# Value bursts of a sliding-window attention kernel: one PSUM bank per array half and step, summed at the evacuation

## The chip, the cores and the metric

The kernel runs on one core of one Trainium2 chip. The metric is the device time of one execution in microseconds; of each kernel the median of several runs is given. A profiled execution has its own time, and its span (first to last instruction) is a little shorter than that.

## What is computed

```python
def _A_ref(x, wqkv, wo):                 # 32 heads of 16, window of 256 keys
    qkv = (x @ wqkv).reshape(B, S, 3, H, Dh).transpose(2, 0, 3, 1, 4)
    q, k, v = qkv[0], qkv[1], qkv[2]
    scores = jnp.einsum("bhqd,bhkd->bhqk", q, k) * (Dh ** -0.5)
    mask = (idx[:, None] - idx[None, :] >= 0) & (idx[:, None] - idx[None, :] < W)
    p = _softmax(jnp.where(mask[None, None], scores, -1e9), axis=-1)
    o = jnp.einsum("bhqk,bhkd->bhqd", p, v)
    return o.transpose(0, 2, 1, 3).reshape(B, S, D) @ wo

def _B_ref(x, w_gate, w_up, w_down):
    h = _sigmoid(x @ w_gate) * (x @ w_up)
    return h @ w_down

g = _sigmoid((x * gate_w).sum(-1, keepdims=True))
out = g * _A_ref(x, wqkv, wo) + (1 - g) * _B_ref(x, w_gate, w_up, w_down)
```

x is 2048 x 512 in fp32, the gated branch has 1376 hidden columns.

## The kernel before

The heads are worked in NG = 8 groups of four, the 2048 queries in NB = 16 blocks of 128. The main loop at L902 counts units u, one block of one group each; a step s is four blocks of queries (512) of one group, so a group has the steps c = 0 to 3. In each unit and for each head hh of the four, TensorE gets, in this order:

- `s_part` (L361): scores of query block u, into a PSUM tile `s`; VectorE adds the mask and takes the row maxima (L377);
- `st_part` (L429): transposed scores of the block nine units earlier, into a tile `st`; ScalarE takes the exponential (L443) into `pbuf` or `V`, the homes of the block's probabilities, and GpSimd masks them (L450, L456);
- a turn or several of `turns` (L754): a pair of matmuls, one on either half of the array, of the projections (`pj`), the gated branch (`gu`) or its tail (`tp`).

Most matmuls use 64 of the array's 128 rows, so that two run side by side, one on the lower half (partitions 0 to 63) and one on the upper. PSUM has eight banks: two with the tag `s`, two with `st`, three with `misc`, and `pv`. A tag's banks are handed out in turn, and an engine's instructions stand in the order in which the code records them; the recording layer adds the waits.

Probabilities times values are done in bursts. From unit 17 on there is a long visit each eight units (`visits`, L895; 14 in all, the last at u = 121), at the head of its unit, ahead of `s_part(u, 0)`. It does two steps, s and s + 1. For each key block j, `pv_row` (L482) issues one matmul per head on one half of the array (`half`: the lower or upper 64 keys), with 32 columns of the array per head; a key block meets only the queries of its window, so a row is 64 to 320 columns wide. The sum over j stands in a bank, and both halves add to the same step's bank. `pv_wide` (L498) keeps them apart in time: in the first phase (`turn` 0) the lower half works for step s in bank `pv` and the upper half for step s + 1 in a bank of tag `st`; then TensorE is drained, and in the second phase the halves change banks. One half takes its key blocks backwards, so that the rows that run side by side have like sizes.

While the burst runs, ScalarE and VectorE do other things that are due (L977 to L988: evacuations, the split of two projections in high and low parts, up to five guests). Behind it ScalarE copies the second step's bank to `pbuf[:, 26:28]` (`o_copy`, L526), and, after the first exponential of the unit, the first step's bank to `pbuf[:, 24:26]`; `o_store` (L529) queues five transfers of them. Slots 24 to 29 of `pbuf` are also the home of the probabilities of each block with u % 8 = 4 (`p_home`, L408). The last group's steps have short visits (`pv_part`, L465), which the change leaves alone.

Of the kernel before, what the change touches and what calls it, by code (L numbers as in the profile page):

```python
# [7 lines left out]
F32 = mybir.dt.float32  # L8
# [3 lines left out]
ALU = mybir.AluOpType  # L12
PSUM = bass.MemoryType.PSUM

P = 128
HB = P // 2
# [7 lines left out]
CH = 512  # L24
NC = T // CH
# [41 lines left out]
def gated_mix_kernel(  # L67
# [11 lines left out]
    nc = tc.nc  # L79
# [30 lines left out]
    ps = ctx.enter_context(tc.tile_pool(name="ps", bufs=1, space=PSUM))  # L110
# [34 lines left out]
    with ExitStack() as actx:  # L145
# [316 lines left out]
        evac = []  # L462
# [19 lines left out]
        def pv_row(s, half, j, bank, first):  # L482
            g, c = divmod(s, NC)
            q0 = 8 * c
            a = 2 * j + half
            k, e = max(a, q0) - 2 * j, min(a + 5, q0 + 8) - 2 * j
            for hh in range(HG):
                v = (j * HG + hh) * VW
                w = min(32, NB * HG * VW - v)
                o = (2 * j - q0) * HB  # L490
                mm(  # L491
                    bank[32 * hh:32 * hh + w, o + k * HB:o + e * HB],
                    vt[HB * half:HB * half + HB, v:v + w], p_run(g * NB + j, hh, half, k, e),
                    start=first, stop=False, skip_group_check=True, tile_position=(HB * half, 32 * hh),
                )
            return e - k

        def pv_wide(s, banks):  # L498
            for turn in range(2):
                rows = []  # L500
                for half in range(2):
                    n = (half + turn) % 2
                    c = (s + n) % NC
                    js = list(range(max(0, 4 * c - 2), 4 * c + 4))
                    rows.append([(s + n, half, j, banks[n]) for j in (js if half != turn else js[::-1])])
                sent = [0, 0]
                began = [False, False]
                while rows[0] or rows[1]:
                    half = 0 if rows[0] and (not rows[1] or sent[0] <= sent[1]) else 1
                    row = rows[half].pop(0)  # L510
                    n = pv_row(*row, turn == 0 and not began[half])
                    began[half] = True
                    sent[half] += n
                if turn == 0:
                    nc.tensor.drain()

        def o_take(s, bank):
            g, c = divmod(s, NC)
# [4 lines left out]
                later.append((oT_d[h * DH:(h + 1) * DH, c * CH:(c + 1) * CH], ob[32 * hh:32 * hh + DH]))  # L523
            later.append((sum_d[c, g * HG:(g + 1) * HG], ob.rearrange("(h r) f -> r h f", r=32)[DH]))

        def o_copy(half, bank):  # L526
            nc.scalar.copy(pbuf[:, 24 + 2 * half:26 + 2 * half].rearrange("p c h t -> p (c h t)"), bank)

        def o_store(s):  # L529
            g, c = divmod(s, NC)  # L530
            both = pbuf[:, 24:28].rearrange("p c h t -> p (c h t)")
            for hh in range(HG):
                h = g * HG + hh
                later.append((oT_d[h * DH:(h + 1) * DH, c * CH:(c + 2) * CH], both[32 * hh:32 * hh + DH]))
            later.append((
                sum_d[c:c + 2, g * HG:(g + 1) * HG].rearrange("c h f -> h c f"),
                both.rearrange("(h r) (c f) -> r h c f", r=32, c=2)[DH],
            ))
# [175 lines left out]
        def proj_sum(s):  # L714
# [12 lines left out]
                lambda k, h=None, x=False, a=(f, c, w): gu_mm(*a, k, h, x),  # L727
# [174 lines left out]
        for u in range(N):  # L902
            if u == LAG:
# [3 lines left out]
                pbuf = ppool.tile([P, 30, HG, HB], F32, name="pbuf")  # L907
# [51 lines left out]
            for hh in range(HG):  # L959
                wide = visits.get(u) == 2  # L960
                if hh == 0 and u in visits:
                    s2 = (u - PVLAG) // 4 - wide
                    if wide:
                        second = ps.tile([P, CH], F32, tag="st", name=f"pv{s2}", bufs=2)
                        pv_wide(s2, (pv, second))
                    else:
                        pv_part(s2, pv)
                if hh == 3 and mid(u + 1):
                    max_split((u - 4) // 4)
                if hh == 0 and mark:  # L970
                    if not mid(u):
                        max_split((u - 5) // 4)
                    run_dmas(later)
                    later.clear()
                    max_store((u - 5) // 4)
                if hh == 0 and wide:
                    flush(evac)  # L977
                    ripe = [held.pop(0) for _ in range(2) if held and held[0] // 2 == u // 8 + 1]
                    for s4 in ripe:
                        proj_hi(s4)  # L980
                    max_load((u - 5) // 4)
                    for s4 in ripe:
                        proj_lo(s4)
                    run_dmas(later)
                    later.clear()
                    for guests, n in ((acts, 2), (behind, 3)):
                        for _ in range(min(n, len(guests))):
                            guests.pop(0)()  # L988
                    o_copy(1, second)
                    evac.append(lambda s2=s2: (o_copy(0, pv), o_store(s2)))  # L990
                elif hh == 0 and u in visits:
                    evac.append(lambda s2=s2: o_take(s2, pv))
                if hh == 2 and mark:
                    transfers()
                if u < NU:
                    s_part(u, hh)
                if 0 <= u - LAG < NU:
                    st_part(u - LAG, hh ^ 1 if u < NU else hh)
                if u < LAG:
                    flush(behind)  # L1000
                    if hh % 2 == 1:
                        upto = n_first * (2 * u + 1 + hh // 2) // (2 * LAG)
                        run_first(upto - done)
                        done = upto
                else:
                    long = u < U_WIDE
                    k8 = (u - LAG) % WIDE * HG + hh
                    dense = GAPS2[max(0, k8 - 1)] < 3 if long else u < NU and (u - PVLAG) % 4 == 3 and hh > 0
                    k = (u - PVLAG) % 4 * HG + hh
                    free = hh == 2 and not mid(u + 1) if long else k in (1, 5, 9) or k in (3, 7) and len(behind) > 2  # L1010
                    guest = behind and (u < PVLAG or u >= NU or free)
                    if guest:
                        behind.pop(0)()
                    if evac and not (NB * NWIDE + LAG <= u < NU and (guest or hh == 3 and mid(u + 1))):
                        evac.pop(0)()
                    elif acts and not dense and (u < NU or hh % 2 == 1):
                        acts.pop(0)()
                if u >= LAG and (hh % 2 == 1 or u < NU) and (u + 1 not in visits or hh < HG - 1):
                    if u < N - 2:
                        next(slots)  # L1020
# [204 lines left out]
```

## Time and profile before

| | |
|---|---|
| median of 3 runs | 717.32 us (717.19 to 717.95) |
| the profiled execution | 716.68 us, span 714.9 us |
| granted TensorE clock, mean | 1.000 |
| TensorE matmuls busy | 707.9 us (99%) |
| TensorE weight loads busy | 608.4 us (85%) |
| VectorE busy | 478.8 us (67%) |
| ScalarE busy | 426.8 us (60%) |
| GpSimd busy | 172.0 us (24%) |

The profile comes from one execution. PE stands for TensorE's matmuls, PEld for its weight loads, DVE for VectorE, ACT for ScalarE, POOL for GpSimd, SP for the queue that issues the transfers. Matmuls are pipelined: a matmul's row lasts longer than the time it adds to the stream, so starts are to be compared, not durations summed. "q" behind an engine's name is its sequencer.

### The profile page before, as it was taken

The page shows a single profiled execution, that of the slowest core. Times are in us where ns is not written, and L with a number is a line of the kernel's source. Part 1 is how long each engine was busy: PE and PEld are TensorE (multiplying, and loading weights), DVE is VectorE, ACT ScalarE, POOL GpSimd, SP SyncE. Part 2 cuts the span into 40 slices and gives each one's busy share as a digit, 9 for nine tenths or more (in the row PEclk, how much of TensorE's full clock was granted, in tenths as well). Part 3 has the DMA queues.
Part 4 walks back from the last instruction along what each step waited for, and adds up shares of the span by engine and source line. Part 5 has one row for each costly group of instructions (what it writes and reads, how often), then busy time and mean ns, then how long its engine had stood idle before and what let it go on. Part 6 is the DMA issues. An engine that isn't in the chain of part 4 may idle for free.

```text
span 714.9 us, 19859 instructions
## 1 busy us (share of the span) xinstructions
PE 707.9 (99%) x7530; PEld 608.4 (85%) x7530; DVE 478.8 (67%) x1455; ACT 426.8 (60%) x890; POOL 172.0 (24%) x254
## 2 busy tenths in 40 slices
PE   9999999999999999999999999999999999999997
PEld 7888889889898898888988888898888888888886
DVE  5368767667676676766667667676747858667481
ACT  6423767667676676766767667775676645435341
POOL 5200333233233233323324323332341000000000
PEclk9999999999999999999999999999999999999999
DMA  8466644635445365462655617564569968779531
GB/s 305 115 192 200 212 130 173 222 128 192 160 171 190 125 206 175 158 210 96 213 166 183 208 49 244 182 230 115 167 207 268 254 177 219 190 188 236 146 65 59
DMA packets 102975, 127.37 MB, mean 178 GB/s; under 512 B 45766, under 2 KB 62662, under 8 KB 102880
## 3 DMA queue, kind: packets, MB, share of 16 engines
q1 hardware_dynamic: 102736, 125.98, 58.0%
q8 instruction: 59, 0.97, 0.6%
q14 instruction: 36, 0.29, 0.1%
q10 hardware_dynamic: 144, 0.13, 0.1%
HBM read 71.80 MB, written 51.13 MB: 172 GB/s over the span
## 4 chain that ended last, share of the span: by engine, by line
PE 99%; issue 0%; DVE 0%; DVEq 0%
PE gu L283 28%; PE pj L283 12%; PE pv L491 9%; PE s L371 6%; PE st L436 6%; PE tp L661 6%; PE pd L96 5%; PE pd L97 5%; PE pd L95 5%; PE vh L698 4%; PE pa L95 2%; PE pa L97 2%; PE pa L96 2%; PE vps L560 2%; PE pv L474 1%; PE pd L1152 1%
## 5 line engine op out<-in xcount | busy, mean ns | idle before, releaser
L377 DVE CUSTOM_DVE_ANT_0 junk<-s,mask 128x384 f32<-128x384 f32 (+2 forms) x512 | 271.8, 531 | 133.7 <-PE s L371 71.5
L283 PE MATMUL gu<-xh,w 64*128 64x512 f32 x1152 | 271.4, 391 | 0.0
L443 ACT ACTIVATE pbuf<-st 128x384 f32<-128x384 f32 (+2 forms) x344 | 166.3, 492 | 70.4 <-PE st L436 38.8
L283 PE MATMUL gu<-xl,w 64*128 64x512 f32 x576 | 183.1, 389 | 0.0
L436 PE MATMUL st<-ring 64*128 64x384 f32 (+2 forms) x536 | 165.6, 326 | 0.0
L371 PE MATMUL s<-ring 64*128 64x384 f32 (+2 forms) x536 | 163.1, 322 | 0.0
L283 PEld LDWEIGHTS gu<-xh,w 64*128 64x128 f32 x1152 | 153.2, 184 | 6.5
L450 POOL TENSOR_SCALAR_AFFINE_SELECT pbuf<-pbuf 128x512 f32<-128x512 f32 x86 | 58.1, 676 | 277.9 <-ACT pbuf L443 247.6
L371 PEld LDWEIGHTS s<-ring 64*128 64x128 f32 x536 | 94.9, 184 | 15.7 <-issue 3.1
L436 PEld LDWEIGHTS st<-ring 64*128 64x128 f32 x536 | 95.5, 184 | 4.0 <-PE pv L474 0.4
L443 ACT ACTIVATE V<-st 128x384 f32<-128x384 f32 (+2 forms) x168 | 73.0, 441 | 33.3 <-PE s L371 20.7
L283 PEld LDWEIGHTS gu<-xl,w 64*128 64x128 f32 x576 | 89.5, 184 | 1.6
L283 PE MATMUL pj<-xl,wqh 64*128 64x512 f32 (+1 forms) x228 | 79.3, 389 | 0.0
L283 PE MATMUL pj<-xh,wqh 64*128 64x512 f32 (+1 forms) x228 | 79.3, 389 | 0.0
L283 PE MATMUL pj<-xh,wql 64*128 64x512 f32 (+1 forms) x228 | 69.7, 389 | 0.0
L96 PE MATMUL pd<-ring,hb 128*128 128x512 f32 x160 | 62.3, 389 | 0.0
L97 PE MATMUL pd<-ring,hb 128*128 128x512 f32 x160 | 62.3, 389 | 0.0
L95 PE MATMUL pd<-ring,hb 128*128 128x512 f32 x160 | 62.3, 389 | 0.0
L91 ACT CAST hb<-V 128x512 fp32r<-128x512 f32 x40 | 24.9, 622 | 59.5 <-DVE V L861 45.8
L456 POOL TENSOR_SCALAR_AFFINE_SELECT pbuf<-pbuf 128x512 f32<-128x512 f32 x84 | 56.0, 667 | 0.0
L491 PE MATMUL pv<-pbuf,V 64*32 64x320 f32 (+4 forms) x1568 | 51.5, 356 | 2.0 <-issue 1.2
L450 POOL TENSOR_SCALAR_AFFINE_SELECT V<-V 128x512 f32<-128x512 f32 x42 | 28.0, 668 | 74.0 <-ACT V L443 72.2
(134 smaller groups left out, 1256.5 us busy)
## 6 DMA issues: line engine op xcount, KB each, us to landing
gu_scratch<-sp SPq DMA_DIRECT2D x72, 256.0 KB
V<-gu_scratch SPq DMA_DIRECT2D x36, 512.0 KB
ring<-stack_scratch SPq DMA_DIRECT2D x56, 256.0 KB
stack_scratch<-sh SPq DMA_DIRECT2D x14, 512.0 KB
stack_scratch<-sl SPq DMA_DIRECT2D x14, 512.0 KB
ring<-stack_scratch SPq DMA_DIRECT2D x14, 512.0 KB
guraw<-in_wgu_dram SPq DMA_DIRECT2D x18, 256.0 KB
v_scratch<-V SPq DMA_DIRECT2D x4, 1088.0 KB
```

The source lines that it names most:

```text
L95: mm(ps, lh, rh, start=first, stop=False)
L96: mm(ps, lh, rl, start=False, stop=False)
L97: mm(ps, ll, rh, start=False, stop=last)
L283: return mm(pt, (wl if w == 2 else wh)[r, d], (xl if w == 1 else xh)[r, d, c * CH:(c + 1) * CH], start=k == 0 and not second, stop=k == 3 ...
L371: mm(pt[:, (k - k0) * P:(e - k0) * P], lhsT, blk(g, k, hh, 1, e - k), start=k == k0, stop=e == i + 1, skip_group_check=True,)
L377: nc.vector.tensor_tensor_reduce(junk[:, 0:n], pt[:, 0:n], mask[:, 3 * P - n:], scale=1.0, scalar=NEG, op0=ALU.add, op1=ALU.max, accum_out ...
L436: mm(pt[:, (q - j) * P:(e - j) * P], lhsT, blk(g, q, hh, 0, e - q), start=q == j, stop=e == last, skip_group_check=True,)
L443: exps.append(nc.scalar.activation(out, pt[:, 0:n * P].rearrange(seen, t=HB, **({} if len(out.shape) == 3 else {"k": 2})), AF.Exp, scale=S ...
L450: nc.gpsimd.affine_select(buf[:, s0:s0 + 2], buf[:, s0:s0 + 2], pattern=[[HB, 2], [0, HG], [1, HB]], compare_op=ALU.is_ge, fill=0.0, base= ...
L456: nc.gpsimd.affine_select(old, old, pattern=[[-HB, 2], [0, HG], [-1, HB]], compare_op=ALU.is_gt, fill=0.0, base=0, channel_multiplier=1,)
L491: mm(bank[32 * hh:32 * hh + w, o + k * HB:o + e * HB], vt[HB * half:HB * half + HB, v:v + w], p_run(g * NB + j, hh, half, k, e), start=fir ...
L661: return mm(tp[b][:, 0:TW], (xl if w == 1 else xh)[r, d, b * P:(b + 1) * P], tw[d][int(w == 2)][r, 0:TW], start=k == 0 and not second, sto ...
```

## The change

`pv_wide` has no phases any more. Each half runs through the rows of step s and then those of step s + 1, key blocks in rising order, the two halves interleaved by the columns sent; there are four banks, one per step and half, and the drain is gone. The lower half has `pv` and one of tag `st`, the upper half the two of tag `s`. `o_copy` becomes `o_sum`: ScalarE copies the lower half's bank to its home in `pbuf`, VectorE adds the upper half's bank to it (where c = 0 the upper half has nothing for the first 64 queries, so it adds 448 columns there). Both steps' copies and sums are recorded behind the burst's guests and ahead of `s_part(u, 0)`.

```diff
         def pv_wide(s, banks):
-            for turn in range(2):
-                rows = []
-                for half in range(2):
-                    n = (half + turn) % 2
+            rows = [[], []]
+            for half in range(2):
+                for n in range(2):
                     c = (s + n) % NC
-                    js = list(range(max(0, 4 * c - 2), 4 * c + 4))
-                    rows.append([(s + n, half, j, banks[n]) for j in (js if half != turn else js[::-1])])
-                sent = [0, 0]
-                began = [False, False]
-                while rows[0] or rows[1]:
-                    half = 0 if rows[0] and (not rows[1] or sent[0] <= sent[1]) else 1
-                    row = rows[half].pop(0)
-                    n = pv_row(*row, turn == 0 and not began[half])
-                    began[half] = True
-                    sent[half] += n
-                if turn == 0:
-                    nc.tensor.drain()
+                    j0 = max(0, 4 * c - 2)
+                    rows[half].extend((s + n, half, j, banks[n][half], j == j0) for j in range(j0, 4 * c + 4))
+            sent = [0, 0]
+            while rows[0] or rows[1]:
+                half = 0 if rows[0] and (not rows[1] or sent[0] <= sent[1]) else 1
+                sent[half] += pv_row(*rows[half].pop(0))
...
-        def o_copy(half, bank):
-            nc.scalar.copy(pbuf[:, 24 + 2 * half:26 + 2 * half].rearrange("p c h t -> p (c h t)"), bank)
+        def o_sum(s, n, banks):
+            home = pbuf[:, 24 + 2 * n:26 + 2 * n].rearrange("p c h t -> p (c h t)")
+            some = slice(0 if (s + n) % NC else HB, CH)
+            nc.scalar.copy(home, banks[0])
+            nc.vector.tensor_tensor(home[:, some], banks[1][:, some], home[:, some], op=ALU.add)
...
                     if wide:
-                        second = ps.tile([P, CH], F32, tag="st", name=f"pv{s2}", bufs=2)
-                        pv_wide(s2, (pv, second))
+                        banks = [[pv], []]
+                        for n, tag in ((0, "s"), (1, "st"), (1, "s")):
+                            banks[n].append(ps.tile([P, CH], F32, tag=tag, name=f"pv{s2}_{tag}{n}", bufs=2))
+                        pv_wide(s2, banks)
...
-                    o_copy(1, second)
-                    evac.append(lambda s2=s2: (o_copy(0, pv), o_store(s2)))
+                    for n in range(2):
+                        o_sum(s2, n, banks[n])
+                    o_store(s2)
```

What the change moves on TensorE is seen at the first long visit (u = 17, steps 0 and 1). Before, from the last scores ahead of the burst through the end of its first phase to the first scores behind it; `pv_869` is the bank `pv`, `pv0_1327` the one of tag `st`, "x3" are three more heads:

```order
L371 MATMUL s16_3_1318<-ring_63 128x128 [waits DVE_49]
L436 MATMUL st7_2_1322<-ring_63 128x384 [waits Activation_49]
L491 MATMUL pv_869<-pbuf_868,V_71 32x128 [waits DMAHW7_49,Pool_49]
L491 MATMUL pv_869<-pbuf_868,V_71 32x128 x3
L491 MATMUL pv0_1327<-pbuf_868,V_71 32x128 [waits Activation_49]
...
L491 MATMUL pv0_1327<-V_71 32x192 [waits Pool_49]
L491 MATMUL pv0_1327<-V_71 32x192 x3
...
L491 MATMUL pv0_1327<-V_71 32x128 x4
L371 MATMUL s17_0_1429<-ring_63 128x256 [waits DVE_49]
L436 MATMUL st8_1_1433<-ring_63 128x384 [waits PE_49]
```

And the same place now; `pv0_s0_1327` and `pv0_s1_1329` are the two banks of tag `s` (steps s and s + 1, upper half), `pv0_st1_1328` that of tag `st`:

```order
L491 MATMUL pv0_s0_1327<-pbuf_868,V_71 32x320 [waits DVE_49]
...
L491 MATMUL pv_869<-pbuf_868,V_71 32x128 x4
L491 MATMUL pv0_s1_1329<-pbuf_868,V_71 32x128 [waits DVE_49]
L491 MATMUL pv0_s1_1329<-pbuf_868,V_71 32x128 x3
L491 MATMUL pv0_st1_1328<-pbuf_868,V_71 32x64 [waits Activation_49]
...
L491 MATMUL pv0_st1_1328<-V_71 32x128 x4
L371 MATMUL s17_0_1433<-ring_63 128x256 [waits DVE_49]
L436 MATMUL st8_1_1437<-ring_63 128x384
L283 MATMUL gu0_2_1_1440<-xh_68,w0_70 128x512
...
L371 MATMUL s17_1_1447<-ring_63 128x256 [waits DVE_49]
```

Each step's rows now stand together, the upper half's first rows wait for VectorE (they take the banks of `s16_2` and `s16_3`), and what `s17_0` and `s17_1` wait for on VectorE is now the first and the second sum, whose banks they take.

On ScalarE and VectorE, the same visit. Before, ScalarE:

```order
L605 CAST w0_70<-guraw1_0_1101 128x512 [waits DMAHW2_49,DVE_49]
L527 COPY pbuf_868<-pv0_1327 128x512 [waits PE_49,Activation_49]
L443 ACTIVATE pbuf_868<-st8_1_1433 128x6x64 [waits PE_49,Pool_49]
L527 COPY pbuf_868<-pv_869 128x512 [waits Pool_49]
L443 ACTIVATE pbuf_868<-st8_0_1448 128x6x64 [waits PE_49]
```

Now, ScalarE:

```order
L601 CAST w0_70<-guraw1_0_1101 128x512 [waits DMAHW2_49,DVE_49]
L522 COPY pbuf_868<-pv_869 128x512 [waits PE_49,Pool_49]
L522 COPY pbuf_868<-pv0_st1_1328 128x512 [waits PE_49]
L443 ACTIVATE pbuf_868<-st8_1_1437 128x6x64 [waits PE_49]
L443 ACTIVATE pbuf_868<-st8_0_1451 128x6x64 [waits PE_49]
```

And VectorE, where before the row maximum of `s17_0` stood right behind L603's low part:

```order
L603 TENSOR_TENSOR w0_70<-guraw1_0_1101,w0_70 128x512 [waits DMAHW2_49,Activation_49]
L523 TENSOR_TENSOR pbuf_868<-pv0_s0_1327,pbuf_868 128x448 [waits DMAHW3_49,DMAHW1_49,Activation_49]
L523 TENSOR_TENSOR pbuf_868<-pv0_s1_1329,pbuf_868 128x512 [waits Activation_49]
L377 ISA junk17_0_1435,mx4_1281<-s17_0_1433,mask_153 128x256 [waits PE_49]
L377 ISA mx4_1281 128x1
```

The first step's copy now stands ahead of the unit's first exponential, and its wait for TensorE is for the last reader of the home that it overwrites (the second step's third row). Lines behind L499 have other numbers in the changed kernel. The orders of SP and GpSimd stay as they were.

## Rows read from the trace of the kernel before

**Rows 1.** The page, part 1: busy us (share of the span) and instructions.

```profile
PE 707.9 (99%) x7530; PEld 608.4 (85%) x7530; DVE 478.8 (67%) x1455; ACT 426.8 (60%) x890; POOL 172.0 (24%) x254
```

**Rows 2.** The page, part 4: shares of the chain of waits, by engine and line.

```profile
PE 99%; issue 0%; DVE 0%; DVEq 0%
PE gu L283 28%; PE pj L283 12%; PE pv L491 9%; PE s L371 6%; PE st L436 6%; PE tp L661 6%; PE pd L96 5%; PE pd L97 5%; PE pd L95 5%; PE vh L698 4%; PE pa L95 2%; PE pa L97 2%; PE pa L96 2%; PE vps L560 2%; PE pv L474 1%; PE pd L1152 1%
```

**Rows 3.** Waits: engine, line, waited for, us in total, times, longest.

```profile
PEld s L371 <- DVE mx L377: 2.9, 11, 0.4
```

**Rows 4.** Timeline of TensorE, first long visit: start us, us, engine, line, operation, count [idle before].

```profile
94.03 1.66 PE L491 MATMUL pv<-pbuf,V 64*32 64x128 f32 x52
...
96.53 1.21 PE L491 MATMUL pv<-pbuf,V 64*32 64x64 f32 x48
...
98.83 0.38 PE L371 MATMUL s<-ring 64*128 64x256 f32 x1
98.83 0.44 PE L436 MATMUL st<-ring 64*128 64x384 f32 x1
99.05 0.46 PE L283 MATMUL gu<-xh,w 64*128 64x512 f32 x2
...
99.81 0.28 PE L371 MATMUL s<-ring 64*128 64x256 f32 x1
```

**Rows 5.** Timeline of TensorE, second long visit.

```profile
123.77 1.66 PE L491 MATMUL pv<-pbuf,V 64*32 64x128 f32 x52
...
127.33 0.45 PE L491 MATMUL pv<-V 64*32 64x320 f32 x4
...
127.60 0.45 PE L491 MATMUL pv<-V 64*32 64x320 f32 x4
...
128.67 0.32 PE L371 MATMUL s<-ring 64*128 64x128 f32 x1
...
129.65 0.22 PE L371 MATMUL s<-ring 64*128 64x128 f32 x1
```

**Rows 6.** Timeline of TensorE's weight loads, second long visit.

```profile
123.40 0.18 PEld L371 LDWEIGHTS s<-ring 64*128 64x128 f32 x1
...
126.33 0.63 PEld L491 LDWEIGHTS pv<-pbuf,V 64*32 64x32 f32 x48 [0.34 <-issue]
```

**Rows 7.** Timeline of TensorE from 123.76 to 123.85 alone: the burst's first matmuls.

```profile
123.77 0.34 PE L491 MATMUL pv<-pbuf,V 64*32 64x128 f32 x8
```

**Rows 8.** Timeline of VectorE, second long visit.

```profile
123.26 0.08 DVE L377 DVE_READ_ACCUMULATOR2_ANT mx<- 128x1 f32 x1
...
123.97 0.08 DVE L377 DVE_READ_ACCUMULATOR2_ANT mx<- 128x1 f32 x1
124.20 0.56 DVE L377 CUSTOM_DVE_ANT_0 junk<-s,mask 128x384 f32<-128x384 f32 x1
...
129.20 0.56 DVE L377 CUSTOM_DVE_ANT_0 junk<-s,mask 128x384 f32<-128x384 f32 x1 [2.62 <-PE s L371]
```

**Rows 9.** Timeline of ScalarE, second long visit.

```profile
128.77 0.59 ACT L527 COPY pbuf<-pv 128x512 f32<-128x512 f32 x1 [3.56 <-PE pv L491]
```

**Rows 10.** Timeline of ScalarE, first long visit.

```profile
99.02 0.59 ACT L527 COPY pbuf<-pv 128x512 f32<-128x512 f32 x1 [2.85 <-PE pv L491]
```

**Rows 11.** Timeline of ScalarE from 94.5 to 95.0.

```profile
94.52 0.61 ACT L307 CAST sh<-pr 128x512 fp32r<-128x512 f32 x1
```

**Rows 12.** Timeline of VectorE from 94.5 to 95.3.

```profile
95.16 0.72 DVE L311 TENSOR_TENSOR sl<-pr,sh 128x512 fp32r<-128x512 f32 x1 [0.35 <-ACT sh L307]
```

**Rows 13.** Groups of VectorE by line and shape: count | busy us, mean ns | idle before.

```profile
L311 DVE TENSOR_TENSOR sl<-pr,sh 128x512 fp32r<-128x512 f32 x27 | 20.0, 778 | 3.2 <-ACT sh L307 3.2
...
L705 DVE TENSOR_TENSOR V<-vh,vsum 128x512 f32<-128x512 f32 x9 | 6.2, 685 | 0.0
```

**Rows 14.** Timeline of VectorE, thirteenth long visit.

```profile
456.49 0.62 DVE L653 TENSOR_TENSOR tail_wql<-tailraw,tail_wqh 128x450 fp32r<-128x450 f32 x1
```

**Rows 15.** Timeline of TensorE, thirteenth long visit.

```profile
457.85 0.38 PE L371 MATMUL s<-ring 64*128 64x256 f32 x1
```

## The prediction, made before the changed kernel ran

> **What bounds the kernel now.** I read the page's busy shares first, then its chain of waits, then the timeline of single long value bursts, since the change touches nothing else. TensorE is busy for 707.9 of 714.9 us [rows 1], and the chain that ended last runs over TensorE for 99% of the span; the value matmuls at L491 are 9% of it [rows 2]. So whatever lengthens or shortens TensorE's stream by a microsecond does so to the kernel. Waits of TensorE on VectorE for a score bank come to 2.9 us in the whole run, in 11 places [rows 3]: the score banks come free in time now, mostly.
>
> There are 14 long visits (u = 17, 25, ... 121), of two kinds that alternate. Seven have steps c = 0 and 1 (kind A, the first at u = 17), seven have c = 2 and 3 (kind B, the first at u = 25). A burst's work I count in units: 64 columns, four heads, two passes (an fp32 matmul leaves two in the trace). For c = 0 the lower half of the array has 5+5+4+2 = 16 units and the upper 5+5+3+1 = 14; every other step has 20 on either half.
>
> In kind A the burst runs from 94.03 to the first score matmul at 98.83, 4.80 us, its second phase beginning at 96.53 [rows 4]. In kind B it runs from 123.77 to 128.67, 4.90 us [rows 5]. Between the phases the weight loads stop for 0.34 us [rows 6]: the drain. A five-unit row's two passes begin at 127.33 and 127.60 [rows 5], so a unit takes 2 x 0.27 / 5 = 0.108 us (0.1076 with one more digit). Eight matmuls, four heads on each half, begin within 0.09 us [rows 7], inside the 0.11 that one pass of these two-unit rows lasts, and A and B take nearly the same time though A has 70 half-units and B 80: a phase lasts as long as its longer half, 20 units in all four cases.
>
> **The change, part by part.** *The burst gets shorter.* Without phases each half runs through its own rows. The second phase of A shows what a run costs beyond its units: 98.83 - 96.53 = 2.30, less 20 units (2.15), leaves 0.15. Then A takes 36 units, 3.87 + 0.15 = 4.02, and saves 0.78. B takes 40 units, 4.30 + 0.15 = 4.45, and saves 0.45. Over seven of each: 5.5 + 3.1 = **8.6 us gained**. That the rows of the two halves are no longer of like size (1 beside 2 units, 3 beside 4) I cost at nothing; the bound above that is a rival, below.
>
> *A wait before the burst.* The upper half's first rows now write the score bank that s(u-1, 2) used, which VectorE must have read. In B its read ends at 123.97 + 0.08 = 124.05 [rows 8], and a weight load follows such a read by 0.06 (123.26 + 0.08 to 123.40, [rows 6, 8]). So it comes at 124.11 where it could have come at about 123.80. The rows behind it stand in the same sequencer: 0.31 us in each B, **2.2 us lost**. In A, VectorE's reads are of 128 or 256 columns and end before the burst; nothing. The other score bank is wanted in mid-burst, after its read (124.20 + 0.56) is over.
>
> *A wait behind the burst.* This decides. Two score banks and one transposed-score bank now hold sums. Let S be the moment of the first score matmul. Now s(u, 1) follows at S + 0.98 (98.83 to 99.81 and 128.67 to 129.65, [rows 4, 5]). After the change it needs the second score bank, which is free when ScalarE has copied the last step's lower half and VectorE has added the upper. ScalarE's copy begins 0.10 after S in B (128.77 against 128.67) and takes 0.59 [rows 5, 9]; in A it begins 0.19 after [rows 4, 10], but there it waits for two engines, and the new copy for TensorE alone, as in B. From ScalarE's end to VectorE's start takes 0.03 (94.52 + 0.61 to 95.16, [rows 11, 12]). The add itself is not in this trace; the nearest is L705, a bank plus an SBUF tile at 512 columns, 0.685, and the dearest of like size is L311 at 0.778 [rows 13]. I take 0.685. Then 0.06 to the weight load, and 0.10 because that load is no longer hidden (the score matmul right behind the burst lasts 0.38, the next of its shape 0.28, [rows 4]). Sum: 0.10 + 0.59 + 0.03 + 0.69 + 0.06 + 0.10 = 1.57, which is 0.59 later than 0.98. TensorE's order puts the transposed scores and the value of three turns behind that matmul, so all of them wait: 14 x 0.59 = **8.3 us lost**.
>
> s(u, 0) waits too, for the sum of the first step. That step is complete in mid-burst, but its copy goes to a home (slots 24 and 25 of `pbuf`) that block j = 4 or 12 still occupies, so it waits for the third row of the second step. In B that row is the upper half's 31st unit: 0.03 + 0.31 + 3.34 = 3.68 after the burst's start; copy from 3.88, add to 5.19, load at 5.25, where S would be 4.76. These 0.49 lie inside the other wait (0.49 + 0.98 = 1.47, under 1.57). One exception: in the thirteenth visit VectorE works on guests until 456.49 + 0.62 = 457.11 [rows 14], where S, now 457.85 [rows 15], moves to 457.07. Its first sum ends at 457.80, s(u, 0) waits 0.79, s(u, 1) comes at S + 1.77: **0.2 us lost**.
>
> *What costs nothing.* The 28 copies stay on ScalarE, one of each two moved from behind the burst into it. The 28 sums are 19.2 us more for VectorE, which has 2.62 us idle ahead of 129.20 [rows 8]; its row maximum of s(u, 0) moves behind the second sum and ends some 0.6 us ahead of s(u, 2), which needs its bank. The orders of SP's and GpSimd's instructions do not change, and the transfers of a visit are queued where they were.
>
> Sum: 2.2 + 8.3 + 0.2 - 8.6 = **+2.1 us**. The profiled execution took 716.68, so it would take 718.8; the median of the three runs is 717.32, and I give the forecast on that: **719.4 us**. (About 0.2%, 1.4 us, is what a measurement of this kernel tells from no change: 715.9 to 718.75 is "same".)
>
> Bounds of the unknown prices: the add at 0.78 gives +1.3, the copy's start at 0.19 gives +1.3; the weight load hidden after all gives -1.4, no cost at all beyond a run's units but 0.10 gives -0.7. So the forecast's own range is 717.3 to 722.0.
>
> **The rivals.** *Faster: most of the wait behind the burst hides.* The place is s(u, 1), the price 0.59 a visit. Were it nothing, the time would be 719.4 - 8.3 = 711.1; from a chain of 1.32 instead of 1.57 downward the kernel would be faster by more than 0.2% (2.1 - 14 x 0.25 = -1.4). For it: every duration in the chain is an engine's occupied time, and a bank might be handed on earlier than its end. Against it: VectorE's starts and TensorE's weight loads in the rows follow the ends, by 0.03 and 0.06. At half the wait, 715.2. Chance 0.14.
>
> *Slower by far: rows of unlike size hold one another up.* If a row could not begin before the second pass of the row ahead of it in program order, the pairs that are matched now lose little, but the new order, worked through row by row, would take 4.52 instead of 3.87 in A and 4.57 instead of 4.30 in B: +0.65 and +0.27, or 6.4 us, 725.8. For it: nothing in the old bursts pairs unlike rows for long. Against it: the upper half's first pass begins with the lower's, well ahead of the lower's second [rows 7], and scores of 256 and 384 columns run side by side at 98.83 with the next turn's matmuls 0.22 behind them [rows 4]. [...] Chance 0.12.
>
> *The change does not do what it says:* the halt in mid-burst stays, for another reason than the drain instruction (a row that waits there for a bank or a mask). Then 0.27 to 0.34 a visit, some 4.3 us, are not gained: 723.7. The order shows no drain there, and the only wait at that place is for banks read long before. Chance 0.05.
>
> **How the numbers follow.** The forecast has 0.66 and the rest, 0.03, is for what I have not seen. Of the forecast's 0.66, its centre 0.65 above the bound of "same", I put 0.38 above it and 0.28 within. Faster: 0.14 and a little, 0.15. Same: 0.30. Slower: 0.38 + 0.12 + 0.05, 0.55. For 8 in 10 the range takes in the forecast's own, half of the faster rival and the smaller part of the slower ones: 715.8 to 722.8.
>
> **What would show it.** Right, if in the profile after: the bursts of A take about 4.0 us and of B about 4.75 with their wait; no gap of 0.3 in the weight loads at mid-burst; VectorE's sums take about 0.69; and behind each burst TensorE's weight load of s(u, 1) is released by the sum, some 1.5 us after the last value row, with an idle stretch of about half a microsecond. Wrong, if s(u, 1) comes at S + 1.0 (then it is faster), or if the halves' rows lag and the bursts stay over 4.5 in A (then the second rival holds).

## The result, and the profile after

The changed kernel takes 720.23 us in the median of five runs (720.15 to 721.08), the kernel before 717.19 beside it (716.64 to 717.95): ratio 1.0044, interval 1.003 to 1.0059. It is slower by 3.0 us; the forecast was slower by 2.1, at 719.4 us, and the range holds the result.

The profiled execution of the changed kernel took 721.08 us, 4.40 more than that of before. Of this, 0.81 us stand ahead of the first long visit (94.84 against 94.03, [rows 4]), where no edit lies; 3.23 lie between the bursts of the first and of the last long visit, the rest behind. Parts 1 and 4 of its page, and its waits, to hold against [rows 1 to 3]:

```profile
PE 708.4 (98%) x7530; PEld 618.1 (86%) x7530; DVE 496.4 (69%) x1483; ACT 431.3 (60%) x890; POOL 172.0 (24%) x254
...
PE 96%; DVE 2%; ACT 1%; issue 0%; DVEq 0%; ACTq 0%
```

```profile
PE s L371 <- DVE pbuf L523: 5.5, 14, 0.5
...
PEld s L371 <- DVE pbuf L523: 12.1, 25, 0.7
...
PEld s L371 <- DVE mx L377: 2.6, 10, 0.4
...
PEld pv_s L491 <- DVE mx L377: 0.9, 5, 0.2
```

TensorE's matmuls are as busy as they were, but VectorE and ScalarE now stand in the chain. A wait that did not exist holds the score matmuls, for VectorE's sum at L523: 14 times the matmuls themselves stand idle, once a visit, and 25 times a weight load comes late. A small one stands ahead of the bursts (`pv_s <- mx`). TensorE's timeline in the first long visit (kind A):

```profile
94.84 0.47 PE L491 MATMUL pv<-pbuf,V 64*32 64x320 f32 x4
...
96.37 0.29 PE L491 MATMUL pv<-pbuf,V 64*32 64x128 f32 x4
...
96.61 0.29 PE L491 MATMUL pv_st<-pbuf,V 64*32 64x64 f32 x4
...
97.09 0.47 PE L491 MATMUL pv_st<-pbuf,V 64*32 64x320 f32 x2
...
98.17 0.41 PE L491 MATMUL pv_st<-V 64*32 64x256 f32 x2
...
98.75 0.30 PE L491 MATMUL pv_st<-V 64*32 64x128 f32 x3
99.36 0.38 PE L371 MATMUL s<-ring 64*128 64x256 f32 x1 [0.31 <-DVE pbuf L523]
...
100.45 0.38 PE L371 MATMUL s<-ring 64*128 64x256 f32 x1
...
101.42 0.28 PE L371 MATMUL s<-ring 64*128 64x256 f32 x1
```

The halt in mid-burst of [rows 6] is gone. The last value row begins 3.94 us after the first; before, it was 4.60. But s(u, 0), which would come 4.15 after the burst's start (the run without sums, below, shows it), comes at 4.52, s(u, 1) 1.09 behind it instead of 0.98, and s(u, 2) 0.97 behind that. What they waited for is in the timelines of ScalarE and VectorE in the same visit, and in the weight loads:

```profile
98.06 0.59 ACT L522 COPY pbuf<-pv 128x512 f32<-128x512 f32 x1 [1.08 <-PE pv_s L491]
99.09 0.59 ACT L522 COPY pbuf<-pv_st 128x512 f32<-128x512 f32 x1 [0.44 <-PE pv_st L491]
```

```profile
98.68 0.62 DVE L523 TENSOR_TENSOR pbuf<-pv_s,pbuf 128x448 f32<-128x448 f32 x1 [0.33 <-ACT pbuf L522]
99.71 0.69 DVE L523 TENSOR_TENSOR pbuf<-pv_s,pbuf 128x512 f32<-128x512 f32 x1 [0.40 <-ACT pbuf L522]
```

```profile
99.36 0.18 PEld L371 LDWEIGHTS s<-ring 64*128 64x128 f32 x1 [0.58 <-DVE pbuf L523]
...
100.45 0.18 PEld L371 LDWEIGHTS s<-ring 64*128 64x128 f32 x1 [0.39 <-DVE pbuf L523]
```

A copy of 0.59, 0.03 to VectorE, a sum of 0.62 or 0.69, 0.05 to the weight load: 98.68 + 0.62 = 99.30 and the load at 99.36; 99.71 + 0.69 = 100.40 and the load at 100.45. In kind B (second long visit) the chain is the same, and the upper half starts late; TensorE's matmuls, its weight loads and VectorE's sums there:

```profile
124.58 0.32 PE L491 MATMUL pv<-V 64*32 64x64 f32 x8
124.91 0.31 PE L491 MATMUL pv_s<-V 64*32 64x128 f32 x4
...
130.04 0.32 PE L371 MATMUL s<-ring 64*128 64x128 f32 x1 [0.48 <-DVE pbuf L523]
...
131.02 0.22 PE L371 MATMUL s<-ring 64*128 64x128 f32 x1
```

```profile
124.91 0.13 PEld L491 LDWEIGHTS pv_s<-V 64*32 64x32 f32 x5 [0.18 <-DVE mx L377]
...
130.91 0.18 PEld L371 LDWEIGHTS s<-ring 64*128 64x128 f32 x1
```

```profile
129.29 0.69 DVE L523 TENSOR_TENSOR pbuf<-pv_s,pbuf 128x512 f32<-128x512 f32 x1 [1.92 <-ACT pbuf L522]
130.17 0.69 DVE L523 TENSOR_TENSOR pbuf<-pv_s,pbuf 128x512 f32<-128x512 f32 x1 [0.18 <-ACT pbuf L522]
```

The first upper row begins 0.33 us behind the first lower one, released by VectorE's read of s(u-1, 2). Behind the burst it is the first sum that costs the time here: s(u, 0) waits for it. The weight load of s(u, 1) follows the second sum by 0.05 (130.17 + 0.69 = 130.86), but its matmul comes 0.98 behind that of s(u, 0), the distance that it has in the kernel before, so the second sum adds nothing to the wait; the other six B visits have 0.98 to 0.99.

From the first matmul of one burst to that of the next, in ns against the kernel before (read from the trace's starts; the first interval begins with an A visit, the last with an A visit; the run without sums is the first experiment, the best version the last):

```
visit                A     B     A     B     A     B     A     B     A     B     A     B     A
after               -4  +568   -95  +781   -80  +583  +203  +500   -62  +393   -83  +576   -53
no sums           -657  +106  -712   +16  -707   +34  -626   -20  -712   +18  -735    -5  -683
best version      -719  +131  -861  +789  -732   +78  -525   -67  -707   -33  -615   +75  -660
```

So an A visit gains what it loses, and a B visit loses half a microsecond.

### The profile page after: what moved, and what is told of

Its sections match the earlier page's. It is cut to its first block, busy times and chain, and to the rows that moved or that the text cites. A ratio compares the mean times of both kernels' runs of the same rounds, so it can differ in the third digit from the quotient of the medians.

```text
span 719.4 us, 19935 instructions
## 1 busy us (share of the span) xinstructions
PE 708.4 (98%) x7530; PEld 618.1 (86%) x7530; DVE 496.4 (69%) x1483; ACT 431.3 (60%) x890; POOL 172.0 (24%) x254
## 4 chain that ended last, share of the span: by engine, by line
PE 96%; DVE 2%; ACT 1%; issue 0%; DVEq 0%; ACTq 0%
PE gu L283 28%; PE pj L283 12%; PE s L371 7%; PE st L436 6%; PE tp L657 6%; PE pd L96 5%; PE pd L97 5%; PE pd L95 5%; PE vh L694 3%; PE pv L491 3%; PE pv_s L491 2%; PE pa L95 2%; PE pa L97 2%; PE pa L96 2%; PE vps L556 2%; PE pv L474 1%
## 5 line engine op out<-in xcount | busy, mean ns | idle before, releaser
L377 DVE CUSTOM_DVE_ANT_0 junk<-s,mask 128x384 f32<-128x384 f32 (+2 forms) x512 | 271.8, 531 | 97.9 <-PE s L371 44.1
L283 PEld LDWEIGHTS pj<-xh,wql 64*128 64x128 f32 (+1 forms) x228 | 41.5, 185 | 1.6
```

Source lines behind the costliest of these rows:

```text
L283: return mm(pt, (wl if w == 2 else wh)[r, d], (xl if w == 1 else xh)[r, d, c * CH:(c + 1) * CH], start=k == 0 and not second, stop=k == 3 ...
L377: nc.vector.tensor_tensor_reduce(junk[:, 0:n], pt[:, 0:n], mask[:, 3 * P - n:], scale=1.0, scalar=NEG, op0=ALU.add, op1=ALU.max, accum_out ...
```

## The experiments

Each starts from the changed kernel; the order of TensorE's value rows stays as it is there, but in the run with the drain. Ratios are to the kernel before, which took 717.0 us in the first four, 717.25 in the next four and 717.3 in the last four.

**The sums left out.** The two banks of a step are written as in the changed kernel, but only the lower one is read.

```diff
             nc.scalar.copy(home, banks[0])
-            nc.vector.tensor_tensor(home[:, some], banks[1][:, some], home[:, some], op=ALU.add)
```

> Leaves out VectorE's 28 sums, so the upper half's part of the long visits' result is missing from the output. Theory (the score banks are held until a sum has read them, about 0.59 us at each of 14 visits, 8.3 us): with no reader the banks are free at once, 720.2 - 8.3 = about 712, and TensorE's weight load of s(u, 1) stands about 1.0 us behind that of s(u, 0), with no idle stretch. Rival (rows of unlike size hold one another up inside the burst): the bursts are as they were, about 720. Rival (the sums load VectorE): about 712 as well; the next run parts these two.

Measured: 712.0 us (711.77 to 712.24), ratio 0.9929 (0.9914 to 0.9944). TensorE's timeline in the first long visit, whose burst begins at 94.40:

```profile
98.55 0.39 PE L371 MATMUL s<-ring 64*128 64x256 f32 x1
...
99.53 0.28 PE L371 MATMUL s<-ring 64*128 64x256 f32 x1
...
100.33 0.28 PE L371 MATMUL s<-ring 64*128 64x256 f32 x1
```

Nothing waits behind the burst; s(u, 0) comes at 4.15, s(u, 1) 0.98 later, s(u, 2) 0.80 behind that. This separates the terms: the bursts with their wait ahead give 717.0 - 712.0 = 5.0 us, and what the sums bring costs 720.2 - 712.0 = 8.2 us.

**The sums kept, the bank let go.** VectorE does the same work at the same place, but reads SBUF alone, so the upper bank is not held for it.

```diff
-            nc.vector.tensor_tensor(home[:, some], banks[1][:, some], home[:, some], op=ALU.add)
+            nc.vector.tensor_tensor(home[:, some], home[:, some], home[:, some], op=ALU.add)
```

> VectorE does 28 sums of the same size at the same places, but of the home with itself, and reads no bank, so the upper half's part is missing from the output. Theory (it is the bank that is held): about 712, as without any sum. Rival (the sums delay VectorE's row maxima, and these delay TensorE): about 720, no gain over the changed kernel.

Measured: 715.0 us (714.12 to 715.3), ratio 0.9968 (0.9957 to 0.9979). That lies between the theory and the rival: of the 8.2 us, 720.2 - 715.0 = 5.2 go with the held bank; the other 3.0 are what VectorE's work costs once the bank is let go. The wait list names it:

```profile
PEld s L371 <- DVE mx L377: 7.1, 24, 0.4
```

Without sums this row reads 3.0 us in 11 places. VectorE's timeline and a weight load of the second long visit show the way:

```profile
128.88 0.69 DVE L523 TENSOR_TENSOR pbuf<-pbuf 128x512 f32<-128x512 f32 x1 [0.23 <-ACT pbuf L522]
129.49 0.55 DVE L377 CUSTOM_DVE_ANT_0 junk<-s,mask 128x384 f32<-128x384 f32 x1
129.97 0.08 DVE L377 DVE_READ_ACCUMULATOR2_ANT mx<- 128x1 f32 x1
```

```profile
130.10 0.18 PEld L371 LDWEIGHTS s<-ring 64*128 64x128 f32 x1 [0.27 <-DVE mx L377]
```

The row maximum of s(u, 0) stands behind the second sum and ends at 130.05; s(u, 2), which takes its bank, loads its weights 0.05 later. In the changed kernel this lies under the longer wait of s(u, 1), and is not seen.

**The engines' roles exchanged.** ScalarE copies the upper half's bank, a score bank, and VectorE adds the lower half's, which is `st` in the first step and `pv` in the second. So the two score banks are free as soon as ScalarE has read them.

```diff
-                        banks = [[pv], []]
-                        for n, tag in ((0, "s"), (1, "st"), (1, "s")):
+                        banks = [[], [pv]]
+                        for n, tag in ((0, "st"), (0, "s"), (1, "s")):
...
-            nc.scalar.copy(home, banks[0])
-            nc.vector.tensor_tensor(home[:, some], banks[1][:, some], home[:, some], op=ALU.add)
+            nc.scalar.copy(home[:, some], upper[:, some])
...
+            nc.vector.tensor_tensor(home[:, some], lower[:, some], home[:, some], op=ALU.add)
```

> Same result as the changed kernel, other parts for the engines: ScalarE copies the upper half's bank (tag s), VectorE adds the lower half's, and the lower half has the bank of tag st for the first step and pv for the second. Theory: the last score bank is free when ScalarE's copy ends, 0.10 + 0.59 + 0.06 = 0.75 us behind the first score matmul, ahead of the 0.98 at which s(u, 1) wants it; the sum that comes 0.7 later holds only pv, which nobody wants for eight units. About 712, 5 below the kernel before. The wait ahead of kind B's bursts stays, 2.2 us in all. Rival (unlike rows): about 720. Rival (the transposed-score bank becomes the next wait, held by the first step's sum): 0.3 to 0.6 a visit, 716 to 720.

Measured: 715.68 us (714.97 to 716.81), ratio 0.9982 (0.9973 to 0.9992): 4.5 us below the changed kernel, and below the kernel before, but 3.7 over the theory's 712. s(u, 0) and s(u, 1) wait for nothing, but `PEld s <- DVE mx` is 6.8 us in 23 places, as in the run before: VectorE's price stays.

**The drain put back** between the two steps' rows, banks as in the changed kernel.

> The changed kernel with the drain between the two steps' rows, all else as it is. If the drain itself was worth what the rows of before say (0.27 to 0.34 us a visit), 720.2 + 4.3 = about 724.5. If the gain of the change came from evening out the halves alone, 720.2 to 721.

Measured: 724.29 us (723.39 to 724.67), ratio 1.0098 (1.0083 to 1.0113), 4.1 us over the changed kernel. The weight loads stop in mid-burst of the first visit as they did before:

```profile
96.27 0.14 PEld L491 LDWEIGHTS pv_st<-pbuf,V 64*32 64x32 f32 x5 [0.37 <-ACT sh L307]
```

(The engine named there is only what ended last.) So the drain is worth 4.1 / 14 = 0.29 us a visit.

**The second sum behind two maxima, and behind four.** Roles exchanged; the second step's sum reads `pv`, which nobody writes for eight units, so it can wait. In the second run `hh == 3`.

```diff
                 if u < NU:
                     s_part(u, hh)
+                if wide and hh == 1:
+                    o_add(s2, 1, banks[1])
+                    o_store(s2)
```

> The roles of the engines are exchanged as in the run with the exchanged roles (715.7 us), and the second step's sum, which reads a bank that nobody wants for eight units, is put behind the maxima of s(u,0) and s(u,1) on VectorE. Theory (what VectorE's sums cost is the maxima that they push back): the wait of s(u,2) on a maximum shrinks, and the time comes near the run without sums (712.0 us): 712 to 713.5 us. Rival (VectorE is simply too full there, and a later sum pushes the later maxima back by as much): 715 to 716 us, with the waits at s(u,3) and behind.

> The same, but the second step's sum behind all four maxima of the unit. Theory: 712 to 713.5 us, nothing waits at s(u,2) and s(u,3). Rival (too full): 715 to 716 us, with the waits in the next unit.

Measured: 714.31 us (713.0 to 716.7), ratio 0.9959 (0.9948 to 0.997), and 721.51 us (720.14 to 722.15), ratio 1.0056 (1.0041 to 1.0071). The first went 1.4 of the 3.7 us to the run without sums, the second missed its theory by 8 us. In both the waits for maxima are down, to 2.6 and 1.7 us, as the theory had it, but new ones stand in the list. Behind two maxima:

```profile
PE st L436 <- DMA ring<-max_scratch: 2.2, 3, 1.6
```

```profile
SPq L345 <- DVE pbuf L529: 19.4, 12, 2.2
```

Behind four:

```profile
PE st L436 <- DMA ring<-max_scratch: 3.5, 4, 1.7
PE st L436 <- ACT pbuf L443: 1.5, 1, 1.5
...
PEld st L436 <- ACT V L443: 2.3, 2, 1.3
...
PEld st L436 <- ACT pbuf L443: 1.9, 1, 1.9
```

```profile
SPq L345 <- DVE pbuf L529: 23.1, 15, 3.9
```

The last row of each is SP's queue: the five stores of a visit stand there until the sum is made (6.9 us at 8 places with the sum in its old place). Behind them in the queue are the loads of the stacks. The transposed scores need those, and the maxima's rows, which are stored and loaded seven to nine us later. SP in the twelfth visit, without sums (the burst begins at 419.43), then with the sum behind four maxima (423.71):

```profile
429.63 3.19 SPq L345 DMA_DIRECT2D ring<-stack_scratch  x5
...
438.60 0.36 SPq L395 DMA_DIRECT2D max_scratch<-nt  x1
441.63 1.18 SPq L402 DMA_DIRECT2D ring<-max_scratch  x2
```

```profile
435.91 3.70 SPq L345 DMA_DIRECT2D ring<-stack_scratch  x5
...
442.91 0.46 SPq L395 DMA_DIRECT2D max_scratch<-nt  x1
448.00 1.18 SPq L402 DMA_DIRECT2D ring<-max_scratch  x2
```

The stacks are loaded 12.2 us after the burst's start instead of 10.2. The maxima's rows are stored at the same place (19.2), but their loads, which wait until that store has landed, go out 5.1 us behind it instead of 3.0, and `st` waits 1.7 us for them. So what comes late is the landing of the maxima's store; no output store stands in the queue at that time any more. That the later stack loads make it land late is argued from these rows, and no run separates it. The waits of the matmuls listed come to 5.0 of the second run's 7.2 us; the two profiled executions are the slowest of each kernel (716.7 and 722.15 us).

**The sums on GpSimd.** ScalarE copies the lower banks too, into SBUF tiles of the tag `sp`, and GpSimd adds.

> Roles exchanged; ScalarE copies the lower banks too, into SBUF, and GpSimd adds there, so VectorE has no sum at all. Theory (the rest of the cost is VectorE's): about 712 us, as without sums. Rival (ScalarE's 28 more copies of 0.59 us push the exponentials back, or GpSimd and VectorE hold one another up at SBUF): 714 to 717 us, with weight loads of st or bursts waiting for ScalarE, or longer operations of VectorE.

Measured: 715.65 us (714.48 to 717.14), ratio 0.9977 (0.9968 to 0.9987): the rival's time. VectorE is back at 478.8 us busy, GpSimd goes from 172.0 to 207.5 for 28 sums (1.27 us on the average), ScalarE to 440.4. What the rival named is hardly seen in the profiled execution, the fastest of nine: VectorE's 512 maxima take 271.8 us, as before, and among its weight loads' waits none above 0.4 us in all is for a copy of a lower bank. So what holds this run at 715.65 stays open.

**Other banks, no wait ahead of the burst.** Step one: lower `pv`, upper `st`; step two: lower `st`, upper `s`; the sum that reads `pv` stands behind two maxima.

```diff
-                        banks = [[], [pv]]
-                        for n, tag in ((0, "st"), (0, "s"), (1, "s")):
+                        banks = [[pv], []]
+                        for n, tag in ((0, "st"), (1, "st"), (1, "s")):
```

> Other banks: the upper half's first step goes to a bank of tag st instead of s, the second step's lower half to the other bank of st; VectorE adds that one first and the first step's sum behind the maxima. It takes the wait ahead of the bursts with 192 rows away (the 0.31 us x 7 = 2.2 us of the prediction). Theory: first upper row of those bursts at once, last row 0.2 to 0.3 us earlier, time 1.5 to 2.2 us below the run with the second sum behind two maxima, if the bank of st comes free in time. Rival: the burst then waits for the exponentials instead, or st(u,1) for the sum: no gain or up to 3 us more.

Measured: 715.37 us (714.62 to 716.88), ratio 0.9978 (0.9968 to 0.9987). TensorE's timeline, fourth long visit (kind B):

```profile
183.08 0.26 PE L491 MATMUL pv<-V 64*32 64x64 f32 x4
183.10 0.31 PE L491 MATMUL pv_st<-V 64*32 64x128 f32 x4
```

The halves start together, and s(u, 0) comes 4.61 us after the burst's start instead of 4.92, here and in all B visits but the first: the 0.31 are real. They are not kept, as VectorE and then the weight load of s(u, 2) show:

```profile
188.45 0.69 DVE L529 TENSOR_TENSOR pbuf<-pv_st,pbuf 128x512 f32<-128x512 f32 x1 [2.57 <-ACT pbuf L522]
189.06 0.55 DVE L377 CUSTOM_DVE_ANT_0 junk<-s,mask 128x384 f32<-128x384 f32 x1
189.53 0.08 DVE L377 DVE_READ_ACCUMULATOR2_ANT mx<- 128x1 f32 x1
```

```profile
189.67 0.18 PEld L371 LDWEIGHTS s<-ring 64*128 64x128 f32 x1
```

The sum, which the next `st` wants, again stands ahead of the maximum of s(u, 0); s(u, 2) comes 0.06 behind that maximum's end.

**The stores a unit later**, in three of these: with the late second sum, on GpSimd, and with the other banks. The stores are now queued at the start of the next unit, where those of the run with the sum behind four maxima stood, instead of at the third head of the visit's own.

```diff
-                    o_store(s2)
...
+            if visits.get(u) == 2:
+                o_store(s2)
             if u < LAG:
```

> Roles exchanged and the second sum behind two maxima, as in the run that gave 714.3 us; besides, the five stores of the outputs are queued one unit later, so that SP's queue does not stand at a store whose sum is not ready, with the loads of the stacks and of the row maxima behind it. Theory (what the late sum cost was the queue: st waited 2.2 us for rows of maxima that came late, and three bursts stopped for 0.27 to 0.41 us): no such wait, no gap inside a burst, 711.5 to 712.5 us, as without sums. Rival (VectorE is too full for the sums wherever they stand): 714 to 715 us again, with waits for maxima in place of those for transfers.

> Sums on GpSimd, as in the run that gave 715.7 us, with the stores queued one unit later. Theory of the queue: the gaps inside bursts go, and the time comes to 711.5 to 713 us. Rival (ScalarE's 28 more copies or GpSimd's own late masks make the difference): it stays at 715 to 716 us.

> Other banks, without the wait ahead of the bursts with 192 rows, as in the run that gave 715.4 us, with the stores queued one unit later. Waits for the maxima remain (s(u,2) 0.25 to 0.37 us late in every visit, s(u,4) in half of them: 4 to 6 us in all against 2.2 us gained ahead of the burst), so both theories expect 714 to 715.5 us; below 713 us would mean that the queue alone had cost it its gain.

Measured: 714.85 us (713.74 to 715.93), ratio 0.9965 (0.9952 to 0.9977); 715.53 us (713.49 to 716.77), ratio 0.9977 (0.9968 to 0.9986); 715.34 us (714.15 to 716.39), ratio 0.9972 (0.9963 to 0.998). None is clearly faster than the run it came from, so the stores' place in the queue is not by itself what kept them from 712. The first has its rival's time, but not the waits for maxima that the rival named (2.2 us in 8 places). It is also to be held against the run with the sum behind four maxima: the stores are at the same place, the sum is made 1.7 us earlier (about 5.8 after the burst's start instead of 7.5 in A, 6.8 instead of 8.5 in B), and the time is 6.7 us less. In it `st <- ring<-max_scratch` has shrunk to one wait of 0.5 us; with what follows from it, 1.0 us stands in a single interval between bursts, the twelfth.

**The maxima's store first.** The first of the three, with one more edit.

```diff
+                    max_store((u - 5) // 4)
                     run_dmas(later)
                     later.clear()
-                    max_store((u - 5) // 4)
```

> The run with exchanged roles, late second sum and held stores (714.9 us median), with one more edit: at each unit that splits maxima, the store of their rows is issued ahead of the other waiting stores on SP's queue (in that run it stood 1.3 us behind a store that waited for a copy, and st then waited 0.5 us, and once a unit later for its exponential 0.8 us). Theory (what is left over the run without sums, 712.0 us, is the round trip of the maxima's rows, which is late in one or two visits of an execution): 712 to 713.5 us, no st waits for rows of maxima, and the runs scatter less than the 2.2 us of that run. Rival (the scatter comes from the transfers' own time, 2.6 us in one run and 3.4 in the other for the same store): 714 to 715 us, still one such wait.

Measured: 713.82 us (713.08 to 714.24), ratio 0.9949 (0.9936 to 0.9963): 1.0 us lower than without the edit, with a spread of 1.2 us instead of 2.2, the two ranges just overlapping; it lies between the theory's range and the rival's. SP now stands at the store of the maxima until they are ready:

```profile
SPq L395 <- DVE nt L392: 109.7, 32, 7.1
```

It was 66.8 us in 24 places. One wait of the transposed scores for such rows is left in the profiled execution (0.2 us, then 0.6 for an exponential), in the interval that the table above shows with +789. This is the fastest version that makes the whole result: 3.5 us below the kernel before and 6.4 below the changed one. It falls 1.8 us short of the run without sums.

## Why the prediction was right

The sign and the mechanism were right, and the place in A; in B another of the two sums is the one that costs. The forecast was 0.9 us too low, and the terms can be told apart.

- **The shorter burst and the wait ahead of it.** Forecast 8.6 - 2.2 = 6.4 us gained; the run without sums gives 5.0. The wait is right: in B the upper half begins 0.33 us behind the lower where the forecast had 0.34 (124.11 against 123.77), and other banks give back the 0.31. The step that was mis-sized is that rows of unlike size were costed at nothing. In the first A visit the lower half takes 97.09 to 98.17 = 1.08 for the ten units of two rows with 320 columns, as forecast; but 94.84 to 96.61 = 1.77 for its first 16 units (16 x 0.1076 = 1.72), and 96.61 to 97.09 = 0.48 for the four units at the start of its second step (0.43). 30 units take 3.33 instead of 3.23. Of these 0.10, 0.08 go between 96.37 and 97.09, where six units in rows of one, two and three stand around the change of step (0.72 instead of 0.65). Over whole bursts, s(u, 0) would come at 4.15 and 4.61 (no wait) where the forecast said 4.02 and 4.45: 0.13 and 0.16 a visit, which is 7 x 0.29 = 2.0 us, and by the medians 1.4. Why the short rows lose this there no run tells.
- **The wait behind the burst.** Forecast 8.3 + 0.2; measured 8.2. The chain stands link by link: copy 0.59, 0.03, sum 0.69 (0.685 was taken), 0.05 to the load (0.06). s(u, 1) comes 0.49 us later than in the run without sums in A, 0.55 in B (0.59 forecast for both). That is 7 x 1.04 = 7.3 us and not the whole: in A the wait at s(u, 1) costs 0.17 more behind it, since s(u, 2) follows by 0.97 where it follows by 0.80 without sums. By the rows it is 7 x (0.66 + 0.55) = 8.5 us. So the sum was met with 0.59 too low for A and too high for B, which is partly luck. The 0.2 of the thirteenth visit did not come: s(u, 1) stands at 5.63 after its burst's start, as in most A visits. Two other A visits had it 0.12 and 0.24 later, since ScalarE's copy began later.
- **s(u, 0)'s own wait** is 0.55 us in B (0.49 forecast), 0.37 in A. In A it is covered, as forecast: s(u, 1)'s moment is set by the second sum, 1.09 behind s(u, 0). In B it is not: there the forecast had the second sum hold s(u, 1) for 0.10 longer than the first one's wait (1.57 against 1.47). The rows show s(u, 1) at 0.98 behind s(u, 0), so the first sum's wait is the whole cost. So the sign that was to show a wrong forecast, s(u, 1) about 1.0 behind the first score matmul, is there in B, but because that matmul itself is 0.55 late.
- **"The 28 sums cost nothing"** was right only as long as s(u, 0) and s(u, 1) wait themselves. By themselves they cost 3.0 us (715.0 against 712.0), because the maxima behind them come late, and with them s(u, 2) (0.05 in the first visit of either kind) and s(u, 3) (0.14 in A, 0.23 in B). The text counted VectorE's idle time ahead of the maximum of s(u, 0), and held that maximum to end 0.6 us ahead of s(u, 2); that held only because s(u, 2) was late itself.
- **The rivals.** In the first visit of either kind no score bank was handed on before its reader ended: the loads follow the sums' ends by 0.05 to 0.06. The halves did not lag: A's burst is 4.15, far below 4.5, and rows of unlike size cost 1.4 to 2.0 us where the second rival had 6.4. With that rival's 4.52 the first score matmul would come 4.67 us behind the burst's start (4.52 + 0.15), and not 4.15. And the halt in mid-burst is gone; put back, it costs 4.1 us (4.3 in the third rival).

What stays open is the 1.8 us between the best version and the run without sums. The waits for maxima that are left (2.2 us in 8 places) are not it, for the run without sums has 3.0 us in 11 places. Of the 1.5 us between the two profiled spans (712.0 and 710.5), 0.45 stand ahead of the first long visit (94.85 against 94.40), where the two differ in the order of one store at most and the profiled executions of all versions scatter from 93.83 to 94.91; 0.84 stand between the bursts by the table above, 0.77 of them in the one interval with +789, the late rows of maxima. No run took that away. Why GpSimd's sums, which leave VectorE as it was, are no better no run shows.

## What to carry to other kernels

Here a score bank was handed on to its next writer only behind a copy of 0.59 us and a sum of 0.69, one after the other. So let the engine that reads first take the bank that is wanted first, and the second one a bank that can wait: that alone was worth 4.5 us here. And work out for each kind of visit which hand-over sets the time: here it was the second sum's in A and the first one's in B. Then look at what stands behind the added work on its engine, and behind its result in the transfer queue: a wait that hides another shows the second one only when it is removed (here the weight loads' waits for maxima, 2.6 us in the changed kernel and 7.1 with the bank let go).

## What the runs showed of the hardware that was not expected

- The two halves of the array, on rows of unlike length, ran almost independently in the changed kernel's first A burst: 30 units in 3.33 us against 3.23 if nothing were lost.
- Sums that were made 1.7 us later, fourteen times, moved the kernel from 714.3 to 721.5 us, though nothing on TensorE reads them: by SP's rows, because the loads behind their stores went out later and the maxima's rows then landed later (argued, not separated).
- The same store of the maxima's rows was waited for 2.6 us in one run (without sums) and 3.4 in another (late sum, held stores), at the same place of the program.
- The 28 sums in SBUF, 21 of 128 x 512 and seven of 128 x 448, took GpSimd 1.27 us on the average in the profile, where VectorE took 0.69 and 0.62 with one operand in a bank.
- After a stop at the weight load of s(u, 1), TensorE took 0.97 us to s(u, 2), where the same stretch takes 0.80 without the stop (run without sums): the wait cost 0.17 more than its own length in kind A, and nothing more in B, where the stop is at s(u, 0) and s(u, 1) follows by 0.98 to 0.99.
